# Layer norm, 32-head attention over one key/value head and an MLP on one core: one buffer for the transformed queries, a fifth set for VectorE's readings, the root by a power, and a new order

## The chip, the cores and the metric

One Trainium2 chip, one of its NeuronCores. The metric is the device time of one launch in microseconds (us), as the median of a few executions. The engines are TensorE (PE in the profile; PEld is its weight load), VectorE (DVE), ScalarE (ACT), GpSimd (POOL) and SyncE (SP, which issues most DMAs). TensorE writes to PSUM, which has eight banks of 512 float32 columns here.

## The reference

```python
def reference(A_x, A_wq, A_wk, A_wv, A_wo, B_x, B_w1, B_w2):
    x = A_x                                    # (1, 2048, 640), bfloat16
    xn = (x - mean(x)) / sqrt(var(x) + 1e-5)   # over the 640 columns
    q = (xn @ wq) as 32 heads of 20            # one key and one value head for all of them
    k, v = xn @ wk, xn @ wv                    # (2048, 20) each
    p = softmax(q k^T / sqrt(20)); o = p v
    return x + concat(o) @ wo + silu(xn @ w1) @ w2      # w1: 640x1728, w2: 1728x640
```

## The kernel before

The 2048 tokens are 16 tiles of 128 rows, and 4 query chunks of 512 columns. Everything is one static program: a list scheduler in the kernel file, run while the program is built, holds planned durations for every operation, plays the engines forward and writes out one list of instructions for each engine with semaphore waits between them. The tables of numbers at the top of the file (SEG, one row for each 32 blocks of work; PRO, the order of the opening jobs; ACT_STATS, NORM_ENG, DT, BATCHES) steer its choices. What stands on the chip is those lists, in their order.

**Opening.** The x tiles arrive by DMA (L1575). Mean and variance come from VectorE's bn_stats (L1685, L1687), or from two ScalarE passes with accumulators for the tiles in ACT_STATS (L1670, L1673, finished by two small VectorE steps, L1676 and L1680). A batch of tiles then gets 1/sqrt(var + eps) by two Newton steps on GpSimd: ten small instructions in a chain (L1734 to L1750), and two more where a GpSimd normalisation needs -mean/sqrt(...) (L1757, L1758). The batches are tiles 0-3, 4-9 and 10-15. The normalisation itself runs on VectorE (L1715) or GpSimd (L1711). Normalised tiles are transposed on TensorE (L1809, job tN) with a copy out by VectorE or ScalarE (L1820, L1817), or by a transposing DMA (L1775) for the tiles in DT. Then come key jobs k0 to k7 (L1828, evicted by L1836, with a second copy kT1 with an offset by GpSimd, L1838), value jobs v0 to v3 (L1851, L1860) and the first query jobs: p0 and p1 are the two halves of the first 128 query columns, q1 the next (all L872). While it waits, TensorE runs matmuls on zeros (L848, L839).

**Attention.** It is 2048 blocks of 128 keys by 512 queries (32 heads, 4 chunks, 16 key tiles). A visit to the scores, S (L1133), is three or four matmuls in 32-row tiles that run beside each other and fill three or four banks; what does not go together goes as one or two. For a block, either ScalarE takes the exponential (L1167, one instruction for one to three adjacent banks), or VectorE makes a 16-bit integer reading of it (L1182) that serves as the exponent bits of a bfloat16, and two shifted copies of this reading are made by integer additions, Y0 and Y1 (L1221 or L1227 on GpSimd, L1215 on VectorE). So a ScalarE block costs one matmul with v (PV, L973), and a VectorE block three. VectorE's readings lie in NZ = 4 sets of three blocks. PV matmuls run four beside each other in 32-column tiles: four matmuls are one slot. Before the wide integer addition is used, GpSimd loads another library (L1242).

**Other work.** Query, MLP and output jobs (L872) are cut into 32-column tiles too, four to a slot. A change of TensorE between row tiles, column tiles and whole-array matmuls is called a switch below. Transformed queries go through `qd` and DMAs (L1345) into qT, which has two buffers, one for even and one for odd chunks; both are first filled with offsets by one DMA each (L1787).

Of the kernel before, what the change touches and what calls it, by code (L numbers as in the profile page):

```python
# [16 lines left out]
P = 128  # L17
# [38 lines left out]
NZ = 4  # L56
# [5 lines left out]
H0_STEP = 10  # L62
# [25 lines left out]
FOUR_FROM = 35  # L88
# [7 lines left out]
PV_HOLD = 12  # L96
# [3 lines left out]
DT = (5, 6, 7, 8, 9, 10, 11, 12, 14, 15)  # L100
NORM_P = 0.9
# [14 lines left out]
K1_ENG = "pool"  # L116
PV_MIN = 3
PV_GO = 9
PRO = "t0 t2 t1 p0 t3 k0 k1 p1 q1 v0 t4 k2 v1 k3 k4 t13 v2 k5 k6 v3 k7 d0"
ACT_STATS = (1, 4, 6, 12, 14, 15)  # L120
NW_ENG = ("pool", "pool", "pool")
NORM_ENG = ("pool", "dve", "dve", "dve", "pool", "dve", "dve", "dve", "dve", "pool", "dve", "pool")
# [71 lines left out]
)  # L194
BATCHES = ((0, 4), (4, 10), (10, 16))
T_ACT = (0, 2, 6)


# [1742 lines left out]
```

## Time and profile before

| | us |
|---|---|
| median of 3 runs (lowest, highest) | 662.92 (662.53, 663.67) |
| the profiled execution, its own time | 662.48 |
| its span, first to last instruction | 660.7 |
| busy: TensorE, ScalarE, VectorE, GpSimd | 654.3, 645.8, 601.5, 420.3 |
| first scores matmul, from the span's start | 17.76 |

Times in the views are counted from the span's start. A busy share of TensorE counts overlapping matmuls once; the ends of matmuls are modelled, so the distance from start to start is the better measure of what one costs. Idle time is put down to the instruction whose end came last.

### The profile page before, as it was taken

To read this page: it belongs to the slowest core of one execution; us is meant where nothing else is said; L and a number is where in the kernel's file an instruction comes from. 1 tells how busy PE (TensorE), PEld (TensorE's weight loads), DVE (VectorE), ACT (ScalarE), POOL (GpSimd) and SP (SyncE) were. 2 spreads that over 40 slices of the span, in tenths; PEclk is the share of its full clock that TensorE was granted. 3 is DMA by queue.
4 is the path that set the end of the run, shared out by engine and by line. 5 is a ranking of instruction groups with operands and counts; after the bars stand their busy time and mean duration, and the time that the engine had idled before them with its cause. 6 is when DMAs were issued, how large, how long until landed. Compare 5 with 4: busy or idle time off the path is not lost.

```text
span 660.7 us, 22924 instructions
## 1 busy us (share of the span) xinstructions
PE 654.3 (99%) x9762; PEld 220.6 (33%) x9764; DVE 601.5 (91%) x1060; ACT 645.8 (98%) x735; POOL 420.3 (64%) x568
## 2 busy tenths in 40 slices
PE   8999999999999999999999999999999999999998
PEld 4432222323333333333333333333332333333334
DVE  7799999899999997999999979999999998999995
ACT  7899999999999999999999999999999999999995
POOL 6646667676776662676666744677666664766673
PEclk9999999999999999999999999999999999999999
DMA  7566300000004200001003210000000310011001
GB/s 212 97 237 195 88 18 11 10 13 13 14 20 72 73 10 10 10 10 18 18 11 57 63 39 10 18 10 8 12 19 10 77 55 25 10 18 34 11 10 42
DMA packets 52058, 27.89 MB, mean 42 GB/s; under 512 B 37910, under 2 KB 51318, under 8 KB 51958
## 3 DMA queue, kind: packets, MB, share of 16 engines
q1 hardware_dynamic: 50502, 26.22, 15.6%
q8 instruction: 78, 1.28, 0.8%
q10 hardware_dynamic: 1456, 0.22, 0.2%
q14 instruction: 22, 0.18, 0.1%
HBM read 11.44 MB, written 2.62 MB: 21 GB/s over the span
## 4 chain that ended last, share of the span: by engine, by line
PE 92%; ACT 3%; DVE 2%; DMA 2%; SPq 1%; issue 0%; DVEq 0%
PE psall L973 34%; PE psall L1133 29%; PE psall L872 27%; ACT sbt L1167 3%; DMA sbt<-sbt 1%; DVE sbt L1685 1%; DMA sbt<-in_A_x_dram 1%; SPq L1575 0%; DVE sbt L1715 0%; PE psall L1828 0%; PE psall L1369 0%; PE psall L1851 0%; ACT sbt L1379 0%; DVE sbt L1467 0%; DVE sbt L1820 0%
## 5 line engine op out<-in xcount | busy, mean ns | idle before, releaser
L1167 ACT ACTIVATE sbt<-psall 128x1024 bf16<-128x1024 f32 (+2 forms) x644 | 609.6, 1068 | 3.5 <-PE psall L1133 2.9
L1221 POOL INT64_ADD sbt<-sbt x491 | 394.1, 815 | 209.1 <-DVE sbt L1182 183.8
L1182 DVE TENSOR_SCALAR sbt<-psall 128x512 int16<-128x512 f32 x739 | 476.4, 684 | 37.1 <-PE psall L1133 27.6
L973 PE MATMUL psall<-sbt 128*32 128x512 bf16 x3526 | 266.7, 383 | 0.0
L1133 PE MATMUL psall<-sbt 32*128 32x512 bf16 x2048 | 243.6, 384 | 0.3 <-ACT sbt L1167 0.2
L872 PE MATMUL psall<-sbt 128*32 128x320 bf16 (+2 forms) x3939 | 218.3, 331 | 0.3 <-DVE sbt L1687 0.3
L1133 PEld LDWEIGHTS psall<-sbt 32*128 32x128 bf16 x2048 | 61.8, 91 | 235.2 <-issue 80.8
L872 PEld LDWEIGHTS psall<-sbt 128*32 128x32 bf16 x3939 | 85.6, 95 | 85.1 <-issue 50.2
L973 PEld LDWEIGHTS psall<-sbt 128*32 128x32 bf16 x3526 | 63.3, 95 | 99.5 <-issue 68.9
L1384 DVE SCALAR_TENSOR_TENSOR sbt<-sbt,psall 128x512 bf16<-128x512 bf16 x54 | 36.7, 682 | 6.5 <-ACT sbt L1379 6.0
L1379 ACT ACTIVATE sbt<-psall 128x512 bf16<-128x512 f32 x54 | 33.6, 629 | 0.4 <-PE psall L872 0.3
L1285 DVE CAST sbt<-psall 128x512 bf16<-128x512 f32 x32 | 21.9, 683 | 0.6 <-PE psall L973 0.4
L1275 DVE TENSOR_TENSOR sbt<-sbt 128x320 bf16<-128x320 bf16 x31 | 15.8, 510 | 0.0
L1448 DVE SCALAR_TENSOR_TENSOR sbt<-psall,sbt 128x320 bf16<-128x320 f32 x28 | 13.5, 484 | 1.6 <-PE psall L872 1.2
L848 PE MATMUL psall<-sbt 128*128 128x512 bf16 (+2 forms) x44 | 12.9, 447 | 1.4 <-DVE sbt L1624 1.2
L1467 DVE SCALAR_TENSOR_TENSOR sbt<-psall,sbt 128x320 bf16<-128x320 f32 x28 | 13.0, 482 | 1.2 <-PE psall L872 1.2
L1336 DVE TENSOR_SCALAR sbt<-psall 128x512 bf16<-128x512 f32 (+1 forms) x19 | 12.9, 678 | 0.1
L1685 DVE BATCH_NORM_STATS2 sbt<-sbt 128x6 f32<-128x320 bf16 x20 | 8.9, 471 | 3.4 <-DMA sbt<-in_A_x_dram 3.4
L1269 DVE RECIPROCAL sbt<-sbt 128x16 f32<-128x16 bf16 x31 | 7.6, 244 | 0.4 <-DMA sbt<-sbt 0.4
L848 PEld LDWEIGHTS psall<-sbt 128*128 128x128 bf16 x46 | 4.8, 112 | 7.5 <-issue 3.3
L1227 POOL TENSOR_TENSOR sbt<-sbt 128x768 int32<-128x768 int32 x4 | 5.9, 1465 | 0.5 <-DVE sbt L1182 0.5
L1464 ACT ACTIVATE sbt<-psall 128x320 bf16<-128x320 f32 x4 | 1.6, 437 | 4.4 <-PE psall L872 4.3
(72 smaller groups left out, 90.8 us busy)
## 6 DMA issues: line engine op xcount, KB each, us to landing
sbt<-in_A_x_dram SPq DMA_DIRECT2D x32, 160.0 KB, 3.7
out_dram<-sbt SPq DMA_DIRECT2D x15, 160.0 KB, 2.0
sbt<-in_B_w_dram SPq DMA_DIRECT2D x5, 432.0 KB, 5.3
sbt<-sbt SPq DMA_DIRECT2D x105, 20.0 KB
sbt<-in_B_w_dram SPq DMA_DIRECT2D x13, 160.0 KB, 3.0
sbt<-sbt SPq DMA_DIRECT2D x1, 1024.0 KB, 6.3
sbt<-sbt SPq DMA_TRANSPOSE x57, 2.5
sbt<-in_A_wo_dram SPq DMA_DIRECT2D x5, 160.0 KB, 3.0
```

What stands on the lines that cost most here:

```text
L848: return pe.matmul(self.bk(b, 0, n), self.zero[:, 0:P], self.zero[:, 0:n], start=True, stop=True)
L872: ins = pe.matmul(self.bk(b, 0, n, r, r + SLOT), w[:, r:r + SLOT], x, start=start, stop=stop, tile_position=(0, r), skip_group_check=True)
L973: ins = pe.matmul(self.bk(ub[k], 0, QW, r, r + SLOT), self.v[:, it.w, it.kt, :], it.x(), start=f, stop=False, tile_position=(0, r), skip_g ...
L1133: ins = pe.matmul(self.bk(bank[x]), self.kT[r:r + SLOT, kk, kt * P:(kt + 1) * P], self.qT[r:r + SLOT, g % 8, (g // 8) % 2, :], start=True, ...
L1167: return a.activation(self.E[:, b0 * QW:(b0 + na) * QW].rearrange("p (b n) -> p b n", n=QW), src, AF.Exp, scale=ACT_SCALE)
L1182: return v.tensor_scalar(self.Z[:, zs, zp * QW:(zp + 1) * QW], self.bk(bb), 0.0, ZMAX, ALU.max, ALU.min)
L1221: sc.new("pool", tp, lambda v, k=k, c=c: v.int64_add(self.Y[:, zs, k, 0:w].bitcast(I64), self.Z[:, zs, 0:w].bitcast(I64), c), zk + [("lib" ...
L1275: op = sc.new(eng, 0.067 + 16 * DH / 960.0, lambda v: v.tensor_tensor(dst, ut[:, :, :, 0:DH], rb, ALU.mult), [key, ("rL", up)], [("o", h0 ...
L1285: sc.new("dve", t_dve_ps(QW), lambda v: v.tensor_copy(self.U[:, up, :], self.bk(ub)), [("B", ub)], [("U", up)], prio=U_PRIO, name=f"Uev{g}")
L1379: sc.new("act", t_act(QW), lambda a: a.activation(t, src, AF.Tanh, scale=0.5), [("B", b)], [("tb", tp)], prio=TH_PRIO, name=f"th{c}_{fk}") ...
L1384: sc.new("dve", t_dve_ps(QW), lambda v: v.scalar_tensor_tensor(out=self.hT[0:rows, fk, :], in0=t, scalar=1.0, in1=src, op0=ALU.add, op1=AL ...
L1685: np_("dve", 0.41, lambda v, hf=hf: v.bn_stats(self.st6[:, n, hf, :], x[:, hf * 320:hf * 320 + 320]), self.xkeys(n), [("st6", n, hf)], pri ...
```

## The change

- qT has one buffer in place of two; the queries of the next chunk overwrite it head by head, and the second fill of 1024 KB (L1787) goes. A condition in the builder demands that every score that reads a head's old queries has been issued before the new ones are made.
- NZ is 5: VectorE's readings have a fifth set.
- 1/sqrt(var + eps) is an addition of eps and one power with exponent -0.5 on GpSimd (`root`), in place of ten Newton instructions. GpSimd's normalisation adds -mean and multiplies with the root, so that only a sign change of the mean (`nm`) is needed beside it. The batches become 0-1, 2-3, 4-7, 8, 9-10 and 11-15.
- kT1 is made by VectorE, GpSimd makes six normalisations instead of four, and GpSimd loads its library for the wide additions right after them (with K1_ENG = "dve", `go_wide` is called ahead of the jobs); the four narrow additions L1227 go.
- The two loads of wk and wv are issued by ScalarE after its table load, not before it. ACT_STATS has five tiles instead of six; tile 0, 1 and 3 now have theirs from VectorE.
- Seven tiles are transposed by TensorE and nine by DMA (before six and ten); all tables have new numbers, so the lists are in a new order.

```diff
-NZ = 4
+NZ = 5
-H0_STEP = 10
+H0_STEP = 15
-FOUR_FROM = 35
+FOUR_FROM = 25
-PV_HOLD = 12
+PV_HOLD = 16
-DT = (5, 6, 7, 8, 9, 10, 11, 12, 14, 15)
-NORM_P = 0.9
+DT = (4, 5, 7, 9, 10, 11, 12, 13, 15)
+NORM_P = 0.7
+POW_FIX = 0.45
+POW_COL = 0.145
+AG_NEXT = 3
-K1_ENG = "pool"
+K1_ENG = "dve"
-PRO = "t0 t2 t1 p0 t3 k0 k1 p1 q1 v0 t4 k2 v1 k3 k4 t13 v2 k5 k6 v3 k7 d0"
-ACT_STATS = (1, 4, 6, 12, 14, 15)
-NW_ENG = ("pool", "pool", "pool")
-NORM_ENG = ("pool", "dve", "dve", "dve", "pool", "dve", "dve", "dve", "dve", "pool", "dve", "pool")
+PRO = "t2 t0 t1 p0 t3 k0 k1 p1 q1 v0 k2 t6 k3 v1 t8 k5 k4 k6 t14 v2 k7 d0 v3"
+ACT_STATS = (2, 4, 6, 12, 15)
+NORM_ENG = ("pool", "pool", "dve", "dve", "pool", "dve", "dve", "dve", "pool", "dve", "pool", "pool")
-    (8.178, 1.808, 1.279, 0.2, 2, 4, 1, 2.527, 0.05, 0.93, 0.18, 32, 0.3, 0.573, 10, 6, 2, 54, 24, 30, 6, 0, 1, 0, 99, 0, 2, 0, -9),
+    (4.197, 1.591, 0.708, 0.165, 6, 5, 5, 0.922, 0.05, 0.3, 2.631, 29, 2.57, 0.576, 10, 21, 7, 54, 22, 33, 21, 0, 0, 0, 99, 0, 2, 0, 2.412),
...
-BATCHES = ((0, 4), (4, 10), (10, 16))
-T_ACT = (0, 2, 6)
+BATCHES = ((0, 2), (2, 4), (4, 8), (8, 9), (9, 11), (11, 16))
+T_ACT = (2, 4, 5, 6)
...
-        self.qT = sb([P, HT, 2, QW], BF16)
+        self.qT = sb([P, HT, QW], BF16)
...
+            assert c == 0 or self.bp >= GB * (8 * (c - 1) + (hi - 1) // DH // 4 + 1)
...
-                np_("pool", 0.85, lambda g: g.tensor_scalar(
-                    xa(n), self.xslot(n), self.rstd[:, n:n + 1], self.nb[:, n:n + 1], ALU.mult, ALU.add),
+                np_("pool", 0.87, lambda v: v.tensor_scalar(
+                    xa(n), self.xslot(n), self.nm[:, n:n + 1], self.rstd[:, n:n + 1], ALU.add, ALU.mult),
...
+        def root(a, b_, pr):
+            ve = self.tmp[:, 0, a:b_]
+            h = self.half[:, :]
+            hb = bass.AP(self.half, h.offset, [list(h.ap[0]), [0, b_ - a]])
+            add = np_("pool", 0.2, lambda g: g.tensor_scalar(ve, self.mv[:, a:b_, 1], EPS, None, ALU.add), mvk(a, b_),
+                      [("va", a)], prio=pr, name="eps")
+            add.then = np_("pool", POW_FIX + POW_COL * (b_ - a), lambda g: g.tensor_tensor(self.rstd[:, a:b_], ve, hb, ALU.pow),
+                           [("va", a), ("half",)], [("rs", a)], prio=pr, name="root")
+            add.lock = add.then.lock = True
+            if any(NORM_ENG[n - 4] == "pool" for n in range(max(a, 4), b_)):
+                np_("pool", 0.22, lambda g: g.tensor_scalar(self.nm[:, a:b_], self.mv[:, a:b_, 0], -1.0, None, ALU.mult),
+                    mvk(a, b_), [("nm", a)], prio=pr + 0.01, name="nm").lock = True
```

The lists at three places. TensorE from its first key job to the first scores, before (L1828 are keys, L848 matmuls on zeros, L872 with 256 columns is p1 and with 512 columns q1, L1133 scores):

```order
L1809 MATMUL psall<-sbt 128x128 x5
L1828 MATMUL psall<-sbt 128x256 x5
L848 MATMUL psall<-sbt 128x512
L1828 MATMUL psall<-sbt 128x256 x5
L872 MATMUL psall<-sbt 32x256 x20
L872 MATMUL psall<-sbt 32x512 x20
L1133 MATMUL psall<-sbt 128x512 x6
L1851 MATMUL psall<-sbt 128x20 x20
```

and the same stretch now (L1780, L1799, L851, L875 and L1136 are the lines that were L1809, L1828, L848, L872 and L1133; L1822 was L1851):

```order
L1780 MATMUL psall<-sbt 128x128 x5
L1799 MATMUL psall<-sbt 128x256 x5
L851 MATMUL psall<-sbt 128x512
L851 MATMUL psall<-sbt 128x448
L1799 MATMUL psall<-sbt 128x256 x5
L875 MATMUL psall<-sbt 32x256 x20
L851 MATMUL psall<-sbt 128x512
L851 MATMUL psall<-sbt 128x480
L875 MATMUL psall<-sbt 32x512 x4
L1136 MATMUL psall<-sbt 128x512 x5
L875 MATMUL psall<-sbt 32x512 x16
L1822 MATMUL psall<-sbt 128x20 x17
```

Two matmuls on zeros stand behind p1, and only the first of q1's five slots is ahead of the first scores; the other four stand behind them. Ahead of this stretch, tiles 2, 0 and 1 are transposed in one row of 15, where tile 0 came first and 2 and 1 followed after two matmuls on zeros.

GpSimd at the first root, before (L1780 makes the offsets that qT is filled with, L1734 to L1750 are the Newton chain):

```order
L1649 MEMSET sbt 128x16
L1780 TENSOR_SCALAR sbt<-sbt 128x512
L1734 TENSOR_SCALAR sbt<-sbt 128x4
L1735 TENSOR_SCALAR sbt<-sbt 128x4
L1741 TENSOR_TENSOR sbt<-sbt 128x4
L1748 TENSOR_TENSOR sbt<-sbt 128x4
L1749 TENSOR_SCALAR sbt<-sbt 128x4
L1750 TENSOR_TENSOR sbt<-sbt 128x4
```

and now (L1727 adds eps, L1729 is the power, L1653 and L1657 are small constants, L1754 is the line that was L1780):

```order
L1727 TENSOR_SCALAR sbt<-sbt 128x2
L1729 TENSOR_TENSOR sbt<-sbt 128x2
L1653 TENSOR_TENSOR sbt<-sbt 128x1
L1657 MEMSET sbt 128x16
L1754 TENSOR_SCALAR sbt<-sbt 128x512
L1727 TENSOR_SCALAR sbt<-sbt 128x2
L1729 TENSOR_TENSOR sbt<-sbt 128x2
```

The root of tiles 0 and 1 is ahead of the offsets, that of tiles 2 and 3 behind them; no library load (ISA in the list) stands ahead of a power.

TensorE some 100 blocks into the attention, before (L973 is PV):

```order
L1133 MATMUL psall<-sbt 128x512 x3
L973 MATMUL psall<-sbt 32x512 x8
L1133 MATMUL psall<-sbt 128x512 x3
L973 MATMUL psall<-sbt 32x512 x16
L1133 MATMUL psall<-sbt 128x512 x4
```

and now, at its first visit of four (L1136 scores, L976 PV):

```order
L1136 MATMUL psall<-sbt 128x512 x3
L976 MATMUL psall<-sbt 32x512 x8
L1136 MATMUL psall<-sbt 128x512 x4
L976 MATMUL psall<-sbt 32x512 x8
L1136 MATMUL psall<-sbt 128x512 x3
```

Visits of four blocks begin earlier, and there are more of them over the run.

More of the change, by code (lines that the diff above doesn't have):

```diff
@@ L549, in alloc @@
         self.eps = sb([P, 1], F32)
+        self.half = sb([P, 1], F32)
+        self.nm = sb([P, NT], F32)
         self.cy = sb([P, 2], I32)
@@ L697, in s_reads @@
             c, h = g // 8, 4 * (g % 8) + j
-            k += [("kT1" if x in dvs else "kT", kt // 2), ("kT", kt // 2), ("qb", c % 2, h)] + self.qkeys(c, h)
+            k += [("kT1" if x in dvs else "kT", kt // 2), ("kT", kt // 2), ("qb", 0, h)] + self.qkeys(c, h)
         return k
@@ L1351, in consume @@
                 op.inc_no = len(ops)
-        reads = [("xnT", 4 * c + i) for i in range(4)] + [("wqd", 0), ("wqd", 1), ("qz", c % 2)]
+        reads = [("xnT", 4 * c + i) for i in range(4)] + [("wqd", 0), ("wqd", 1), ("qz", 0)]
         if c >= 2:
@@ L1624, in prologue @@
         np_("dve", 0.3, lambda v: v.memset(self.zero[:, :], 0.0), [], [("zero",)], prio=-1.0, name="zero")
-        pool(0.1, lambda g: g.memset(self.eps[:, :], EPS), [], [("eps",)])
+        pool(0.1, lambda g: g.memset(self.half[:, :], -0.5), [], [("half",)])
         for k in range(2):
@@ L1684, in stats @@
             for hf in range(2):
-                np_("dve", 0.41, lambda v, hf=hf: v.bn_stats(self.st6[:, n, hf, :], x[:, hf * 320:hf * 320 + 320]),
-                    self.xkeys(n), [("st6", n, hf)], prio=prio, name=f"st{n}")
-            np_("dve", 0.10, lambda v: v.bn_aggr(self.mv[:, n, :], self.st6[:, n, :, :]),
-                [("st6", n, 0), ("st6", n, 1)], [("mv", n)], prio=prio - 0.001, name=f"ag{n}")
+                last = np_("dve", 0.41, lambda v, hf=hf: v.bn_stats(self.st6[:, n, hf, :], x[:, hf * 320:hf * 320 + 320]),
+                           self.xkeys(n), [("st6", n, hf)], prio=prio, name=f"st{n}")
+            op = np_("dve", 0.10, lambda v: v.bn_aggr(self.mv[:, n, :], self.st6[:, n, :, :]),
+                     [("st6", n, 0), ("st6", n, 1)], [("mv", n)], prio=prio - 0.001, name=f"ag{n}")
+            if n == AG_NEXT:
+                last.then = op
         def mvk(a, b_):
@@ L1766, in prologue @@
                 self.batch[n] = a
-            newton(a, b_, 0.001 * i if b_ <= 4 else 0.3, NW_ENG[i])
+            root(a, b_, 0.001 * i if b_ <= 4 else 0.3)
             if b_ <= 4:
@@ L1780, in prologue @@
         pool(0.95, lambda g: g.tensor_scalar(self.qo[:, :], self.zero[:, 0:QW], self.offq[:, :], 1.0, ALU.add, ALU.mult),
-             [("zero",), ("offq",)], [("qo",)])
+             [("zero",), ("offq",)], [("qo",)], 0.5)
         tb = self.qo[:, :]
-        def qz(par, extra=()):
-            h0 = 2 if par == 0 else 0
-            rep = bass.AP(self.qo, tb.offset, [list(tb.ap[0]), [0, HT - h0], list(tb.ap[1])])
-            op = sc.dma("sp", lambda q: q.dma_start(self.qT[:, h0:HT, par, :], rep), [("qo",)] + list(extra),
-                        [("qb", par, h) for h in range(4 * h0, H)], P * (HT - h0) * QW * 2, sem=sem(f"qz{par}"))
-            op.inc_no = 1
-            sc.note(op, (), [("qz", par)])
-        qz(0)
+        h0 = 2
+        rep = bass.AP(self.qo, tb.offset, [list(tb.ap[0]), [0, HT - h0], list(tb.ap[1])])
+        op = sc.dma("sp", lambda q: q.dma_start(self.qT[:, h0:HT, :], rep), [("qo",)],
+                    [("qb", 0, h) for h in range(4 * h0, H)], P * (HT - h0) * QW * 2, sem=sem("qz"))
+        op.inc_no = 1
+        sc.note(op, (), [("qz", 0)])
         if W1_LATE:
             load_w1()
-        pool(0.4, lambda g: g.memset(self.w2[:, FC, :], 0.0), [], [("w2z",)])
+        pool(0.4, lambda g: g.memset(self.w2[:, FC, :], 0.0), [], [("w2z",)], 0.5)
         def late_loads(key):
```

73 lines of the change are left out of this document (14 added, 59 removed), and 124 rows, old and new, of the table SEG.

## The prediction

> **What bounds the kernel now.** I read the busy shares first, then busy time by stretch, then single instructions in order of time. The page's first parts:
>
> ```profile
> span 660.7 us, 22924 instructions
> PE 654.3 (99%) x9762; PEld 220.6 (33%) x9764; DVE 601.5 (91%) x1060; ACT 645.8 (98%) x735; POOL 420.3 (64%) x568
> ```
>
> Two engines are nearly full. The stretches (TensorE, its weight load, VectorE, ScalarE, GpSimd, granted clock) tell when:
>
> ```profile
> 0.00:10.00 10.00, 8.83 (x29) 3.51 (x30) 5.69 (x20) 7.31 (x16) 7.39 (x33) 1.00 0.83 229
> 10.00:20.00 10.00, 9.30 (x133) 5.14 (x133) 10.00 (x39) 8.69 (x19) 4.63 (x18) 1.00 0.49 149
> 20.00:30.00 10.00, 9.11 (x101) 4.12 (x101) 7.55 (x20) 8.96 (x11) 6.87 (x20) 1.00 0.55 91
> 30.00:40.00 10.00, 9.70 (x131) 4.05 (x130) 8.79 (x21) 9.45 (x12) 6.95 (x7) 1.00 0.82 265
> 40.00:60.00 20.00, 20.00 (x274) 5.86 (x273) 19.30 (x34) 20.00 (x25) 9.47 (x13) 1.00 0.51 164
> ...
> 100.00:200.00 100.00, 99.90 (x1509) 32.03 (x1509) 94.19 (x159) 100.00 (x107) 71.33 (x88) 1.00 0.06 15
> ...
> 600.00:640.00 40.00, 40.00 (x636) 13.39 (x628) 37.48 (x65) 40.00 (x44) 28.74 (x36) 1.00 0.08 19
> ```
>
> From 40 us on both are at 99 to 100%; only the first 40 us leave TensorE idle, 1.9 us of it between 10 and 40. A busy TensorE may still hide waits inside its overlapping matmuls, so I look at starts, in the timeline of TensorE alone:
>
> ```profile
> 99.78 0.39 PE L973 MATMUL psall<-sbt 128*32 128x512 bf16 x4
> 100.10 0.39 PE L1133 MATMUL psall<-sbt 32*128 32x512 bf16 x3
> 100.42 0.62 PE L973 MATMUL psall<-sbt 128*32 128x512 bf16 x8
> 100.97 0.39 PE L1133 MATMUL psall<-sbt 32*128 32x512 bf16 x3
> ...
> 103.03 0.83 PE L973 MATMUL psall<-sbt 128*32 128x512 bf16 x12
> 103.80 0.40 PE L1133 MATMUL psall<-sbt 32*128 32x512 bf16 x4
> 104.12 0.61 PE L973 MATMUL psall<-sbt 128*32 128x512 bf16 x8
> ```
>
> A visit is followed by PV 0.32 us after its start, whether three scores were issued (100.10) or four (103.80). Rows of 4, 8 and 12 PV matmuls take 0.32, 0.55 and 0.77. So a slot of 512 columns costs 0.222, a visit 0.215, and each switch 0.105: 0.215 + 0.105 = 0.32; 2 x 0.222 + 0.105 = 0.55; 3 x 0.222 + 0.105 = 0.77. A slot of 320 columns follows from the last job:
>
> ```profile
> 654.96 2.63 PE L872 MATMUL psall<-sbt 128*32 128x320 bf16 x72
> ```
>
> Seventeen starts in 2.63 - 0.30 us (0.30 is one matmul's length, below) give 0.137.
>
> ```profile
> L872 PE MATMUL psall<-sbt 128*32 128x320 bf16 x2464 | 116.2, 302 | 0.0
> L1167 ACT ACTIVATE sbt<-psall 128x1024 bf16<-128x1024 f32 x577 | 544.5, 1054 | 2.9 <-PE psall L1133 2.5
> L1167 ACT ACTIVATE sbt<-psall 128x1536 bf16<-128x1536 f32 x44 | 65.1, 1484 | 0.5 <-PE psall L1133 0.4
> L1167 ACT ACTIVATE sbt<-psall 128x512 bf16<-128x512 f32 x23 | 14.2, 624 | 0.1
> L1182 DVE TENSOR_SCALAR sbt<-psall 128x512 int16<-128x512 f32 x739 | 476.4, 684 | 37.1 <-PE psall L1133 27.6 <-PE psall L973 0.5 <-POOL sbt L1221 0.3
> ```
>
> Counted over the order of before from its first scores on, TensorE has 621 visits, 1250 switches, 1251 slots of 512 columns, 616 of 320, and small whole-array work for some 8 us: 133.5 + 131.3 + 277.7 + 84.4 + 8 = 635. Measured from the first scores at 17.76 (below) to the last matmul's end at 657.59 it is 639.8. Rounding a price by 0.002 moves this by 2.5 us, and 1.9 are the early waits. So TensorE runs through its list almost without a stop: its list is the time. ScalarE is full beside it; were its work to grow, it would take over.
>
> **The change part by part: TensorE's list.** The new order has 613 visits (210 rows of four instead of 186), 1230 switches, 1259 slots of 512 columns and as many of 320. Of the eight slots more, three are PV: VectorE now reads 745 blocks instead of 739 (TENSOR_SCALAR instructions in its list), two more matmuls each. The other five are query work, four of them q1's, which stood ahead of the first scores. One tile more is transposed after them: five matmuls, 0.28 (ten took 0.73 from 12.17, five 0.45 from 11.45, below). Matmuls on zeros are about as many. In all -8 x 0.215 - 20 x 0.105 + 8 x 0.222 + 0.28 = -1.72 - 2.10 + 1.78 + 0.28 = -1.8 us.
>
> **The other engines' load.** ScalarE has 18 exponentials over two banks less, 11 over three more and 3 over one less. A two-bank one costs 544.5 / 577 = 0.944 us, a three-bank one 65.1 / 44 = 1.480, a one-bank one 14.2 / 23 = 0.617: -17.0 + 16.3 - 1.9 = -2.6 us, more than TensorE loses. VectorE gets six readings, 6 x 476.4 / 739 = 3.9 us, and eight copies kT1 that the trace shows on GpSimd only. Nearest on VectorE: a one-column step took 0.14 (L1680 at 12.91) and a normalisation of 640 columns 1.46 / 4 = 0.37, so 1.1 to 2.9 for eight, and I take 2. Against 601.5 busy of 660.7 that is under 1%; what hides it is VectorE's idle 59 us. GpSimd is 64% busy and loses work. Its library load now starts right after its normalisations and costs it one wait:
>
> ```profile
> POOL sbt L1242 <- issue: 8.5, 1, 8.5
> ```
>
> PV work of the first group covers it on both sides. One qT buffer adds no wait: a query job is made at the earliest Q_LEAD = 54 visits, 162 blocks, ahead of its use, so 512 - 162 = 350 blocks after the last score that reads the old queries, some 109 us at 639.8 us for 2048 blocks. The fifth set only loosens waits. Both at nothing; should a DMA be late, TensorE's list stops there, since it is in order, and every engine with it.
>
> **The opening.** Its steps before:
>
> ```profile
> 1.17 10.04 PE L848 MATMUL psall<-sbt 128*128 128x512 bf16 x34 [1.17 <-DVE sbt L1624]
> ...
> 4.05 0.72 ACT L1670 ACTIVATE sbt<-sbt 128x640 bf16<-128x640 bf16 x1
> ...
> 5.08 0.89 DVE L1685 BATCH_NORM_STATS2 sbt<-sbt 128x6 f32<-128x320 bf16 x2 [0.66 <-DMA sbt<-in_A_x_dram]
> ...
> 5.54 0.19 ACT L1673 ACTIVATION_READ_ACCUMULATOR sbt<-sbt 128x1 f32 x1
> ...
> 6.36 0.69 POOL L1780 TENSOR_SCALAR sbt<-sbt 128x512 bf16<-128x512 bf16 x1
> ...
> 7.97 0.26 POOL L1734 TENSOR_SCALAR sbt<-sbt 128x4 f32<-128x4 f32 x1 [0.93 <-DVE sbt L1687]
> ...
> 8.56 0.49 DVE L1685 BATCH_NORM_STATS2 sbt<-sbt 128x6 f32<-128x320 bf16 x1 [0.32 <-DMA sbt<-in_A_x_dram]
> ...
> 10.55 0.20 POOL L1750 TENSOR_TENSOR sbt<-sbt 128x4 f32<-128x4 f32 x1
> ...
> 11.00 1.46 DVE L1715 TENSOR_SCALAR sbt<-sbt 128x640 bf16<-128x640 bf16 x4
> ...
> 11.45 0.45 PE L1809 MATMUL psall<-sbt 128*128 128x128 bf16 x5 [0.23 <-DVE sbt L1715]
> ...
> 12.17 0.73 PE L1809 MATMUL psall<-sbt 128*128 128x128 bf16 x10
> ...
> 12.91 0.13 DVE L1680 TENSOR_SCALAR sbt<-sbt 128x1 f32<-128x1 f32 x1
> ...
> 16.02 1.81 PE L872 MATMUL psall<-sbt 128*32 128x256 bf16 x40
> ...
> 16.80 0.47 ACT L1313 ACTIVATE sbt<-psall,sbt 128x256 bf16<-128x256 f32 x1
> ...
> 17.76 0.60 PE L1133 MATMUL psall<-sbt 32*128 32x512 bf16 x6
> ```
>
> Ten Newton steps run from 7.97 to 10.75, then four normalisations, the transposes from 11.45, p1 and q1 from 16.02, ScalarE's eviction of p1 at 16.80, and scores at 17.76, behind q1. Now I follow the new lists with these durations. ScalarE reads tile 2, which lands at 5.08 (VectorE waited for it), in 1.7 us (two passes and two read-outs took from 4.05 to 5.73), so VectorE has its variance at 7.3. GpSimd does the first root at about 6.2, then the offsets (0.69), and starts the second root at 8.1. The power is in no row. Below it can't be under a small GpSimd addition, 0.20 (10.55); above, I let it cost the whole chain, 2.78. I take 0.7, nearer to the small instruction, since it is one of them with more arithmetic. Then the second root ends at 9.1. VectorE normalises tiles 0 and 1 from 7.4, has five readings of tiles 5 and 7 to do (tile 7 lands at 8.56), and normalises 2 and 3 from 9.95. The transposes start at 10.45 instead of 11.45. The matmuls on zeros that stand ahead of them are six fewer, 1.3 us, and cover this to 0.5 us.
>
> From there VectorE copies tiles 0 and 1 out between readings, p0 starts at 12.5, k1 after VectorE's copy of tile 3 at 14.65, p1 at 15.3 (16.02 before), its eviction ends at 16.5, and the first scores start at 16.75: **-1.0 us**. With a power of 0.2 they start no earlier, for VectorE's readings hold tile 2; if all other waits shrink too, -2.0. With 2.78, two of them in a row and the offsets between, tile 2 is normalised at 13.5 and the first scores come at 20.3: +2.5. The early waits of 1.9 us stay, between 0.9 (the transposing DMAs are one fewer and start earlier) and 2.9.
>
> **The sum.** 660.7 - 1.8 - 1.0 = 657.9 of span; the profiled execution took 662.48, so 1.8 more, 659.7. The median is 0.4 above that execution: **660.1 us**, I say 660.0.
>
> **The rivals.**
> - *The opening gains nothing.* The later x tiles set it: tile 7 lands at 8.56 and TensorE waits for transposing DMAs after the first scores. For it: VectorE is 100% busy from 10 to 20 us, and the new lists give it more readings there. Then -1.8 alone or, with one more us of early waits, -0.8: 661 to 662.3, between faster and no change.
> - *Slower: the fourth bank.* Twenty-four more visits hold four banks at once, and TensorE, in order, waits until the engines have emptied them. Weight loads for scores wait on VectorE and ScalarE already, up to 0.5 us at a time, but under running matmuls:
>
> ```profile
> PEld psall L1133 <- DVE sbt L1182: 69.7, 175, 0.4
> PEld psall L1133 <- ACT sbt L1167: 42.5, 106, 0.5
> ```
>
>   If each of the 24 stood still for 0.4 us (69.7 / 175), that is 9.6: 669.6. It counts as slower from 4.2 / 24 = 0.18 each. Against it: 186 visits of four leave TensorE at 100% now, and ScalarE's load falls.
> - *Slower: the power needs code of its own.* The row of L1242 shows 8.5 us for a library. Were a load hidden in the first power, the second root would end near 15.7, the first scores come 4.9 later than before and the sum be 662.9 - 1.8 + 4.9 = 666.0; it decides from about 4 us on. Against it: the lists have an instruction of their own ahead of each library load, and none ahead of a power; the first addition and the last product of the Newton chain took 0.26 and 0.20 (7.97, 10.55), no sign of a load. [...]
>
> **How the numbers follow.** A measurement of this kernel tells about 0.2% from no change, 1.3 us: faster is under 661.6, slower over 664.2. The forecast case has 0.74 and lies at 657.5 to 661.5 (first scores -2.0 to 0, early waits 0.9 to 1.9, switch price 0.1). The first rival has 0.14, half faster and half the same; the fourth bank 0.08; the code load 0.04. So faster 0.74 + 0.07 = 0.81, same 0.07, slower 0.12. The range, 657.5 to 664.0, holds the first two cases and the dear power without code load, and leaves out the slower ones.
>
> **What would show it.** Right: first scores near 16.75, transposes near 10.45, a power under 1 us, TensorE at 100% from 40 us on, and 641 us from the first scores to the end (642.9 before). Wrong: TensorE under 99% in a stretch after 40 us, with score weight loads that wait longer than 0.5 us; or a power of over 2.8 us.

## The result: 2.5 us faster, and the profile after

The changed kernel takes 660.41 us in the median of 20 executions (658.93 to 662.90), the kernel before 662.93 in as many (661.70 to 664.80): a ratio of 0.9963, 95% interval 0.9954 to 0.9973. The forecast was 660.0 in a range from 657.5 to 664.0. The profiled execution of the changed kernel took 659.94 (before 662.48), its span 658.1 (660.7). Two parts of its page, busy time and the costliest groups:

```profile
span 658.1 us, 22878 instructions
PE 649.4 (99%) x9776; PEld 221.9 (34%) x9778; DVE 604.4 (92%) x1075; ACT 642.1 (98%) x721; POOL 417.9 (63%) x543
...
L1170 ACT ACTIVATE sbt<-psall 128x1024 bf16<-128x1024 f32 (+1 forms) x634 | 608.7, 1077 | 4.3 <-PE psall L1136 3.5
```

TensorE lost 4.9 us of busy time and ScalarE 3.7, VectorE gained 2.9. The timeline of the opening, all engines, with the rows that answer to those of before (L1727 adds eps, L1729 is the power, L1719 normalises on VectorE, L1780 transposes, L875 with 256 columns is p0 and p1, L1136 are scores):

```profile
6.08 0.26 POOL L1727 TENSOR_SCALAR sbt<-sbt 128x2 f32<-128x2 f32 x1
6.42 0.74 POOL L1729 TENSOR_TENSOR sbt<-sbt 128x2 f32<-128x2 f32 x1
7.20 1.21 DVE L1719 TENSOR_SCALAR sbt<-sbt 128x640 bf16<-128x640 bf16 x2 [0.24 <-POOL sbt L1729]
...
8.79 0.71 POOL L1729 TENSOR_TENSOR sbt<-sbt 128x2 f32<-128x2 f32 x1
...
10.46 1.01 PE L1780 MATMUL psall<-sbt 128*128 128x128 bf16 x15 [1.57 <-DVE sbt L1719]
...
12.26 0.73 PE L875 MATMUL psall<-sbt 128*32 128x256 bf16 x20
...
14.83 0.73 PE L875 MATMUL psall<-sbt 128*32 128x256 bf16 x20
...
15.61 0.47 ACT L1316 ACTIVATE sbt<-psall,sbt 128x256 bf16<-128x256 f32 x1
...
16.35 0.60 PE L1136 MATMUL psall<-sbt 32*128 32x512 bf16 x5
```

The transposes begin at 10.46 and the first scores at 16.35, 1.41 us earlier than before. TensorE's own timeline shows its two main stops afterwards, early at k6 (L1799) and once near the end:

```profile
29.52 0.39 PE L1136 MATMUL psall<-sbt 32*128 32x512 bf16 x3
31.17 0.71 PE L1799 MATMUL psall<-sbt 128*128 128x256 bf16 x5 [1.26 <-DMA sbt<-sbt]
31.81 0.39 PE L1136 MATMUL psall<-sbt 32*128 32x512 bf16 x3
...
637.88 0.83 PE L976 MATMUL psall<-sbt 128*32 128x512 bf16 x12
639.18 0.40 PE L1136 MATMUL psall<-sbt 32*128 32x512 bf16 x4 [0.47 <-ACT sbt L1170]
```

The same in its stretches (TensorE, weight load, VectorE, ScalarE, GpSimd, granted clock):

```profile
30.00:40.00 10.00, 8.76 (x112) 3.55 (x113) 8.74 (x21) 8.54 (x10) 2.20 (x4) 1.00 0.86 317
40.00:60.00 20.00, 19.96 (x285) 6.49 (x286) 18.95 (x35) 19.85 (x25) 13.22 (x17) 1.00 0.44 127
...
600.00:640.00 40.00, 39.51 (x605) 13.03 (x601) 37.34 (x65) 39.30 (x42) 28.39 (x37) 1.00 0.08 19
```

Where the 2.6 us of span come from is read best from the starts of single scores matmuls in the two traces (L1133 before, L1136 after; the last row but one is the last matmul of all):

```
start of                 before    after   difference
first scores              17.76    16.35      -1.41
129th scores matmul       62.07    61.69      -0.38
1921st scores matmul     613.07   609.70      -3.37
last matmul              657.29   654.75      -2.54
end of the span          660.7    658.1       -2.6
```

Beside it stands the list alone, each instruction at the prediction's prices in the order of the lists: 638.1 us before, 636.1 after, so -2.0 (the prediction's count by groups gave 635 before; rounding moves both sums alike). Of that, +0.4 lies ahead of the 129th scores matmul (42.6 and 43.0) and -2.4 behind it. So up to there -1.41 + 0.4 + 0.63 more of waits = -0.38; from there on -2.4 of list and 0.2 more of waits. Most of what the opening won was spent again by 62 us. Part of the 1.41 was never a gain: four slots of q1, 4 x 0.222 = 0.9 us, moved from ahead of the first scores to behind them. From the first scores to the last matmul the time fell by 1.1 us (639.5 to 638.4): -2.0 of list, +0.8 of waits, the rest rounding.

### The profile page after: what moved, and what is told of

Its sections match the earlier page's. It is cut to its first block, busy times and chain, and to the rows that moved or that the text cites. A ratio compares the mean times of both kernels' runs of the same rounds, so it can differ in the third digit from the quotient of the medians.

```text
span 658.1 us, 22878 instructions
## 1 busy us (share of the span) xinstructions
PE 649.4 (99%) x9776; PEld 221.9 (34%) x9778; DVE 604.4 (92%) x1075; ACT 642.1 (98%) x721; POOL 417.9 (63%) x543
## 3 DMA queue, kind: packets, MB, share of 16 engines
HBM read 11.44 MB, written 2.62 MB: 21 GB/s over the span
## 4 chain that ended last, share of the span: by engine, by line
PE 95%; DVE 1%; POOL 1%; ACT 1%; DMA 1%; issue 0%; DVEq 0%; SPq 0%; POOLq 0%
PE psall L976 35%; PE psall L1136 30%; PE psall L875 28%; ACT sbt L1170 1%; DMA sbt<-sbt 1%; PE psall L851 1%; DVE sbt L1185 0%; PE psall L1799 0%; PE psall L1373 0%; DVE sbt L1719 0%; POOL sbt L1715 0%; DVE sbt L1693 0%; PE psall L1780 0%; PE psall L1822 0%; POOL sbt L1655 0%
## 5 line engine op out<-in xcount | busy, mean ns | idle before, releaser
L1170 ACT ACTIVATE sbt<-psall 128x1024 bf16<-128x1024 f32 (+1 forms) x634 | 608.7, 1077 | 4.3 <-PE psall L1136 3.5
L1224 POOL INT64_ADD sbt<-sbt x494 | 399.1, 820 | 215.3 <-DVE sbt L1185 185.9
L976 PE MATMUL psall<-sbt 128*32 128x512 bf16 x3538 | 267.7, 383 | 0.0
L1136 PE MATMUL psall<-sbt 32*128 32x512 bf16 x2048 | 240.3, 384 | 1.4 <-ACT sbt L1170 0.5
L875 PE MATMUL psall<-sbt 128*32 128x320 bf16 (+2 forms) x3939 | 213.4, 330 | 0.1
L1136 PEld LDWEIGHTS psall<-sbt 32*128 32x128 bf16 x2048 | 61.2, 91 | 234.2 <-issue 97.1
L875 PEld LDWEIGHTS psall<-sbt 128*32 128x32 bf16 x3939 | 86.3, 96 | 82.4 <-issue 45.6
L976 PEld LDWEIGHTS psall<-sbt 128*32 128x32 bf16 x3538 | 63.2, 95 | 100.9 <-issue 70.2
L851 PE MATMUL psall<-sbt 128*128 128x512 bf16 (+3 forms) x41 | 11.4, 422 | 1.3 <-DVE sbt L1632 1.2
L1799 PE MATMUL psall<-sbt 128*128 128x256 bf16 x40 | 5.7, 272 | 1.3 <-DMA sbt<-sbt 1.3
L851 PEld LDWEIGHTS psall<-sbt 128*128 128x128 bf16 x43 | 4.2, 107 | 6.5 <-issue 2.6
L1678 ACT ACTIVATE sbt<-sbt 128x640 bf16<-128x640 bf16 x5 | 3.7, 732 | 2.8 <-DMA sbt<-in_A_x_dram 2.6
```

What stands on the lines that cost most here:

```text
L851: return pe.matmul(self.bk(b, 0, n), self.zero[:, 0:P], self.zero[:, 0:n], start=True, stop=True)
L875: ins = pe.matmul(self.bk(b, 0, n, r, r + SLOT), w[:, r:r + SLOT], x, start=start, stop=stop, tile_position=(0, r), skip_group_check=True)
L976: ins = pe.matmul(self.bk(ub[k], 0, QW, r, r + SLOT), self.v[:, it.w, it.kt, :], it.x(), start=f, stop=False, tile_position=(0, r), skip_g ...
L1136: ins = pe.matmul(self.bk(bank[x]), self.kT[r:r + SLOT, kk, kt * P:(kt + 1) * P], self.qT[r:r + SLOT, g % 8, :], start=True, stop=True, ti ...
L1170: return a.activation(self.E[:, b0 * QW:(b0 + na) * QW].rearrange("p (b n) -> p b n", n=QW), src, AF.Exp, scale=ACT_SCALE)
L1224: sc.new("pool", tp, lambda v, k=k, c=c: v.int64_add(self.Y[:, zs, k, 0:w].bitcast(I64), self.Z[:, zs, 0:w].bitcast(I64), c), zk + [("lib" ...
```

## The experiments

All comparisons are with the changed kernel (660.41; 660.42 in a second series) unless said otherwise; ratios are to the kernel before on the same chip. The planner's order was held fixed in all but the last two.

**The power alone, taken out and put in.** In the changed kernel the power was replaced by the nine small instructions of the Newton chain (the edit, shortened):

```diff
-            add.then = np_("pool", ..., lambda g: g.tensor_tensor(self.rstd[:, a:b_], ve, hb, ALU.pow),
+            add.then = np_("pool", ..., newt,        # bit trick, then twice: y*y, *v, *-0.5+1.5, *y
```

> The changed kernel with its order of instructions held fixed on every engine, and only the power taken back: each of the six roots is an addition and nine dependent small GpSimd instructions (the Newton chain, about 2.8 us) instead of an addition and one power (0.74 us for two columns). Theory (the power moves the opening, TensorE's list carries the rest unchanged): the root of tiles 0 and 1 ends near 8.8 instead of 7.2, the offsets (0.69) come behind it, the root of tiles 2 and 3 ends near 12.3 instead of 9.5, the first transposes start near 12.8 instead of 10.46, and the first scores come near 18.7 instead of 16.35. The end comes later by those 2.3 us, or by up to 2 more where the later roots delay the transposing transfers that k6 waits for: 662.7 to 664.7 us against 660.4. Rival (the opening gains nothing, since the early waits give back what the first scores gain): within 0.7 us of 660.4, with the first scores late and the waits between 17 and 36 us smaller by as much.

669.84 us (668.34 to 671.96; ratio 1.0090, 1.0069 to 1.0111): 9.4 more, outside both theories. TensorE's timeline (L1794 are transposes, L1813 keys; the row at 29.79 is k2):

```profile
13.41 1.78 PE L1794 MATMUL psall<-sbt 128*128 128x128 bf16 x15 [4.62 <-DVE sbt L1719]
...
21.30 0.60 PE L1136 MATMUL psall<-sbt 32*128 32x512 bf16 x5
...
29.79 1.22 PE L1813 MATMUL psall<-sbt 128*128 128x256 bf16 x5 [3.53 <-DMA sbt<-sbt]
...
33.14 0.61 PE L1136 MATMUL psall<-sbt 32*128 32x512 bf16 x3
```

and its stretches, where the granted clock is the column behind GpSimd's:

```profile
12.00:14.00 2.00, 0.59 (x6) 0.59 (x7) 1.09 (x5) 0.00 (x0) 0.63 (x4) 0.50 0.72 246
14.00:16.00 2.00, 2.00 (x15) 1.44 (x13) 1.58 (x6) 1.42 (x3) 0.00 (x0) 0.50 0.00 0
...
38.00:40.00 2.00, 2.00 (x15) 1.07 (x12) 1.75 (x4) 1.02 (x1) 0.00 (x0) 0.50 0.45 99
```

The roots delay the transposes by 2.95 us, near the 2.3 expected. Two things come on top. The later roots are late too, for which the expectation allowed up to 2 us: the first transposing DMA is issued 6.79 us later (SyncE's timeline, the changed kernel and, below, this one):

```profile
16.50 13.86 SPq L1749 DMA_TRANSPOSE sbt<-sbt  x9
```

```profile
23.29 9.16 SPq L1763 DMA_TRANSPOSE sbt<-sbt  x5
```

k2, which doesn't wait in the changed kernel, waits 3.53 us for a transposing DMA. The other I had not in mind: with the waits the clock goes. TensorE runs at half its clock from 10.9 to 17.7 (a visit of three takes 0.61, not 0.39), and again from 28.0 to 41.6. The first scores come 4.95 late, the 41st scores matmul 11.6 in this execution (the slowest of the six, 671.96), and the distance stays 11.6 until the late waits. Of the 11.6, the transposes are 2.95, the clock up to the first scores 2.0, and k2's wait in place of the changed kernel's at k6 2.2 (3.53 - 1.35, its second profile below). The 4.5 that are left I put down to the clock behind k2, by subtraction; so somewhat more than half is the clock.

The reverse, the kernel before with the power in its first root only (the edit in words):

```diff
-  ten GpSimd instructions for the root of tiles 0 to 3
+  eps added, then one power of four columns
```

> The kernel before with its order of instructions held fixed, and only the first root (tiles 0 to 3) made by a power: an addition and one power of four columns (about 1.03 us by the changed kernel's rows) in place of ten small instructions that ran from 7.97 to 10.75. Theory (the power alone gains next to nothing, the new order is needed to use it): the root is done near 9.3, but VectorE's readings of other tiles stand ahead of the four normalisations in its list until 10.97, so these start at 11.00 as before; first scores at 17.5 to 17.8, time within 0.4 us of 662.9. Rival (the chain of small instructions was the bound of the opening): normalisations from 9.6, first scores 1.4 us earlier, 661.5 us.

662.85 (ratio 0.9994, 0.9979 to 1.0008): no gain. VectorE's timeline has the four normalisations (L1732) right behind the reading of another tile, 1.2 us after the power had ended (GpSimd: start 8.59, 1.06 long):

```profile
9.98 0.83 DVE L1702 BATCH_NORM_STATS2 sbt<-sbt 128x6 f32<-128x320 bf16 x2
10.73 0.19 DVE L1704 BATCH_NORM_AGGREGATE sbt<-sbt 128x2 f32<-128x12 f32 x1
10.84 1.46 DVE L1732 TENSOR_SCALAR sbt<-sbt 128x640 bf16<-128x640 bf16 x4
```

So the power is worth nothing in the old order and 9.4 us in the new one: the new order puts two roots and GpSimd's offsets in a row and needs short roots. What an order that was planned for Newton chains from the start would lose was not tried.

**Does TensorE's list hold the time, and alone?** First, less work for ScalarE:

```diff
+                cut = QW if v < 120 else 448      # exponentials on 448 of 512 columns
```

> The changed kernel, its order fixed, with the exponentials of all but the first 120 visits made on 448 of each block's 512 columns (an eighth of the exponentials is left out); TensorE does all that it did. ScalarE's two-block exponential should fall from 1.08 us by about 0.11, some 45 to 50 us over the run. Theory (TensorE's list is the time): 659.4 to 660.4, TensorE still at 99 to 100%, the idle time of ScalarE larger by as much as its work shrinks; only the late waits of about 1 us can go. Rival (ScalarE, busy 98%, is the bound or nearly so): 640 or less.

660.56 (ratio 0.9957, 0.9941 to 0.9973): no gain, as the list theory says. An exponential over two banks takes 0.92 us instead of 1.05, but ScalarE's busy time falls only by 23.8 (642.1 to 618.3), about half of what was expected. Then less for TensorE:

```diff
+                cut = QW if f else 448            # PV matmuls on 448 of 512 columns
```

> The changed kernel, its order fixed, with all PV matmuls but each group's first row made on 448 of 512 columns (an eighth of the weighted sum of values is left out). By the price of a slot (0.222 us for 512 columns, that is 64 columns = 0.027) some 858 slots get shorter, 22.9 us in all. Theory (TensorE's list is the time, and a slot costs what its columns cost): 18 to 23 us less, 637.5 to 642.5, less the full 22.9 where ScalarE, whose exponentials start to start add up to some 613 us, becomes the next bound. Rival (a slot's price is not its columns, or another engine is the bound): 660.

657.39 (ratio 0.9921, 0.9906 to 0.9937): 3.0 less, not 18 to 23. The theory that TensorE's list is the time *alone* falls. The slots did get shorter as expected: two of them and a switch take 0.495 us from start to start in the median, where the changed kernel has 0.548,

```profile
104.24 0.56 PE L977 MATMUL psall<-sbt 128*32 128x448 bf16 x8
104.74 0.39 PE L1137 MATMUL psall<-sbt 32*128 32x512 bf16 x3
```

so a slot is 0.027 shorter, some 23 us over the run, and the list is about 613 us. But from the first scores to the last matmul 634.3 went by, so some 21 us of waits came in where the changed kernel has 2.3. One stretch of each shows it, the changed kernel and, below, this one:

```profile
100.00:200.00 100.00, 99.90 (x1528) 32.23 (x1529) 94.71 (x160) 100.00 (x107) 69.64 (x87) 1.00 0.08 17
```

```profile
100.00:200.00 100.00, 99.08 (x1548) 33.97 (x1540) 95.09 (x161) 100.00 (x108) 69.97 (x87) 1.00 0.10 18
```

ScalarE was at 100% and stays there. Its busy share counts overlapping instructions once, so I look at starts here too: an exponential over one, two or three banks takes 0.477, 0.904 or 1.330 us from start to start in both traces, and with such prices ScalarE's work between 100 and 600 us fills 487 of 500 us in the changed kernel and 489 here. It has little room to follow a faster TensorE. Both cuts at once:

> The changed kernel, its order fixed, with both cuts of the two experiments before at once: exponentials on 448 of 512 columns after the first 120 visits, and PV matmuls on 448 columns (an eighth of exponentials and of the weighted sum is left out). The exponentials alone gained nothing (660.6), the matmuls alone 3 us (657.4), though TensorE's slots had become 27 us shorter by their prices. Theory of two tied engines (TensorE's list is the time and ScalarE stands right behind it, each hides a gain of the other): together they give most of the 27, 633 to 645 us. Rival (a third limit, VectorE's readings or the banks' round trips, holds the time): 652 to 657, as with the matmuls alone.

648.84 (ratio 0.9780, 0.9766 to 0.9795): 11.6 less, between the two forecasts. Of the 27 us in the expectation, starts show 23: the 27 goes by a price for 448 columns that the trace doesn't bear out. Its executions had a mean clock of 0.994 to 0.995 (1.000 is the full clock), and the profile shows half the clock from 31.7 to 38.6 us behind a wait of 1.60 at k6, 3.6 us of delay at the 129th scores matmul against the cut of PV alone. In the same stretch as above:

```profile
100.00:200.00 100.00, 99.37 (x1548) 33.29 (x1540) 96.07 (x163) 97.56 (x109) 70.86 (x88) 1.00 0.07 17
```

So TensorE and ScalarE are tied, and each alone hides a cut of the other. What keeps the last 8 to 11 us of the cut is open: no engine is at 100% here (TensorE 99.37, ScalarE 97.56, VectorE 96.07), and VectorE's readings were not cut.

**The waits.** Two places of TensorE's list were altered, k6 behind the next visit and tile 14's transposes, and one PV row ahead of the visit that waits at 639.18 (the orders, in words):

```diff
-  PV x4, scores x3, k6 x5, scores x3, t14 x5, v2 x20        -  PV x12, scores x4, PV x8
+  PV x4, scores x3, scores x3, t14 x5, k6 x5, v2 x20        +  PV x16, scores x4, PV x4
```

> The changed kernel with two places of TensorE's list altered and nothing else. First, the five matmuls of k6, which waited 1.26 us at 31.17 for their transposing transfer, go behind the next visit of scores and the transposes of tile 14: some 0.65 us of work then stands in the wait, and two switches of 0.105 go. Second, one row of the PV matmuls behind the visit of four at 639.18, which waited 0.47 us for an exponential, goes ahead of it (0.22). Theory (TensorE's list with its few waits is the whole time): 0.6 to 1.1 us less than the changed kernel, 659.3 to 659.8, with the waits at these places smaller by as much. Rival (the waits belong to banks and exponentials, and reappear at the next visit): no change, 660.4, with the same sum of waits at other rows.

660.31 (ratio 0.9957, 0.9942 to 0.9972): no change that can be measured. The rival was right for k6; in TensorE's timeline its wait of 1.26 turned into two (L1163 are scores, L1807 transposes, L1826 k6, L1849 v2):

```profile
30.49 0.40 PE L1163 MATMUL psall<-sbt 32*128 32x512 bf16 x3 [0.56 <-ACT sbt L1197]
30.82 0.45 PE L1807 MATMUL psall<-sbt 128*128 128x128 bf16 x5
31.11 0.71 PE L1826 MATMUL psall<-sbt 128*128 128x256 bf16 x5
32.34 0.66 PE L1849 MATMUL psall<-sbt 128*128 128x20 bf16 x20 [0.52 <-DVE sbt L1834]
```

The earlier visit waits for its banks, and v2 for k6's eviction (L1834). The visit after that starts at 33.02 instead of 33.08. The second place gained a little: the last matmul starts at 654.45 instead of 654.75.

**The clock and the matmuls on zeros.** Ten more of them, in the two longest waits (the edit in words):

```diff
+        extra = {first transposes: 6 matmuls on zeros, k6: 4 matmuls on zeros}
```

> The changed kernel, its order fixed, with ten more matmuls on zeros on TensorE and nothing else: six ahead of the first transposes (TensorE stood idle there from 8.89 to 10.46) and four ahead of k6 (idle from 29.9 to 31.17). They lie in waits, so the order theory expects the same time in an execution at full clock, 659.0 to 660.5. Clock theory, from the two experiments before (idle stretches of 3.5 to 4.6 us, and one of 1.39, were followed by 2.6 to 13 us at half the clock; the changed kernel's executions with a mean clock of 0.995 took 662.6 to 662.9, those at 1.000 took 658.9 to 660.5): with the waits filled, the executions below 0.999 go, the median is 659.7 to 660.2 and the highest under 661.5. Rival (the clock falls for reasons outside these two waits): 3 or 4 executions in 10 stay at 661.3 to 662.9.

> The changed kernel once more, on the same chip as the kernel with the added matmuls on zeros, for the spread of its executions: 660.4 in the median, some 4 in 10 with a mean clock under 0.999 and at 661.3 to 662.9. If the profiled execution is one of those, it shows at which wait the clock falls: by the clock theory right behind the wait at 9 to 10.5 or that at 30 to 31.2.

660.26 (659.51 to 660.51) and, for the changed kernel beside it, 660.42 (659.83 to 662.85, one of seven at a clock of 0.995). The profiled execution of the latter was at full clock; its idle stretch ahead of the transposes was 0.55, not 1.57, though the transposes began at 10.46 again, so the matmuls on zeros take another time from one execution to the next. They start 0.43 us apart until the clock first rises and 0.22 apart afterwards, and it rises at 4.26 in the one profile and at 6.32 in the other. The six added ones overran the wait: transposes at 11.37, first scores at 17.22, 0.88 later than in that second profile; at the last matmul 0.28 of it is left. Once more, and the opposite, six matmuls on zeros fewer:

> The kernel with ten more matmuls on zeros once more, for the spread: the first five executions were all at a mean clock of 0.999 or 1.000 (659.5 to 660.5), while 9 of the changed kernel's 27 were under 0.998. Clock theory: again all at or over 0.999, none above 661. Rival (chance): some 3 in 10 at 661.3 to 662.9.

> The changed kernel, its order fixed, with six fewer matmuls on zeros ahead of the first transposes, so that TensorE stands idle from about 7.5 to 10.46 instead of from 8.89. Clock theory: an idle stretch near 3 us is followed by half the clock for some us, as 4.6 us were; the opening to the first scores and what follows takes 2 to 5 us longer, 662.5 to 665, with a granted clock near 0.5 in the stretch after 10 us in the profile. Rival (the matmuls on zeros only fill time): 660.4, clock 1.00.

With ten more: 660.71 (659.74 to 660.93), again none below 0.999; of the changed kernel's 27 executions 9 were below 0.998. With six fewer: 662.80 (660.79 to 664.28; ratio 0.9984, 0.9972 to 0.9997, where the kernel with ten more had 0.9951, 0.9939 to 0.9964, beside the same runs of before), and all ten executions at 0.994 to 0.997. TensorE's timeline and three stretches of this kernel:

```profile
1.18 6.66 PE L859 MATMUL psall<-sbt 128*128 128x512 bf16 x22 [1.18 <-DVE sbt L1640]
10.46 1.01 PE L1788 MATMUL psall<-sbt 128*128 128x128 bf16 x15 [2.62 <-DVE sbt L1727]
...
17.89 0.60 PE L1144 MATMUL psall<-sbt 32*128 32x512 bf16 x5
...
31.39 0.72 PE L1807 MATMUL psall<-sbt 128*128 128x256 bf16 x5
```

```profile
10.40:11.60 1.20, 1.14 (x17) 1.03 (x18) 1.20 (x5) 1.07 (x4) 0.00 (x0) 0.99 1.06 367
11.60:13.00 1.40, 1.40 (x8) 0.31 (x10) 1.40 (x7) 0.77 (x3) 0.12 (x1) 0.50 0.99 316
13.00:15.00 2.00, 2.00 (x28) 1.30 (x23) 0.85 (x4) 0.82 (x2) 1.83 (x4) 0.50 0.29 104
```

The transposes start on time, but half the clock from 11.6 to 15 makes the first scores 1.54 late. This execution, the fastest of the ten, lost little by it: k6 (L1807 here) starts at 31.39, 0.12 behind the changed kernel's second profile, its wait gone. The six matmuls on zeros are thus worth some 2 us of the median (2.4 against the changed kernel, 2.1 against the kernel with ten more on the same chip), by the clock that they keep up: at a mean clock of 0.995 this kernel and the changed one both take 662.9 in the median. The ten more make the time steadier, not lower. If the rate of 9 in 27 held, none in ten would come by chance about once in 60 times, an estimate; on the one chip that ran both kernels the changed one had only one in seven. No kernel here that does the whole work is measurably faster than the changed one.

**The fifth set and the visits of four, undone one at a time.** Here the planner writes a new order.

```diff
-NZ = 5
+NZ = 4
```

> The changed kernel with four sets for VectorE's readings instead of five, everything else as changed. The planner then writes another order: 627 visits of scores instead of 613, 1262 switches instead of 1230, 1299 slots of 512 columns instead of 1259, by the prices of the prediction a list of 654.3 us against 636.1. Theory (the list is the time): 18.2 us more than the changed kernel, 677 to 680 us. Rival (the fifth set matters by the waits that it takes away, and the counts do not add up to the time): within 5 us of 660, or far above 680 with TensorE waiting.

690.03 (ratio 1.0413, 1.0398 to 1.0428): 29.6 more, of which the list explains 18.2. From the first scores to the last matmul 667.9 us pass for a list of 654.3, so waits are 13.6 instead of 2.3, and they grow with the length of the run (5.5 at the middle of the scores). One stretch:

```profile
200.00:300.00 100.00, 99.12 (x1563) 35.53 (x1564) 89.14 (x151) 93.53 (x105) 58.91 (x74) 1.00 0.11 28
```

ScalarE and VectorE have room there, against 100 and 95 in the changed kernel's stretch above. And part of the list is itself waiting. L842 are matmuls on zeros, which the planner puts where it expects TensorE to wait (the changed kernel and, below, this one):

```profile
L842 PE MATMUL psall<-sbt 128*32 128x512 bf16 x1 | 0.4, 379 | 0.0
```

```profile
L842 PE MATMUL psall<-sbt 128*32 128x512 bf16 (+7 forms) x40 | 11.9, 339 | 0.0
```

At a slot's price the 39 more are 8.7 of the 18.2 us. With the 11.3 of other waits (13.6 - 2.3), about 20 of the 29.6 us are waits, planned for or not; the 14 visits and 32 switches more are 6.4 by price. So the rival was right in large part: the fifth set matters by the waits that it takes away. And the limit for visits of four:

```diff
-FOUR_FROM = 25
+FOUR_FROM = 35
```

> The changed kernel with visits of four scores allowed from the 35th on as before, instead of the 25th; the planner writes another order, with 629 visits instead of 613 and 1265 switches instead of 1230: by the prices a list of 644.7 us against 636.1. Theory (the list plus waits like the changed kernel's): 669 us; with waits that grow as with four sets (the list 18 us longer, the time 30), up to 676. Rival (a visit of four costs more than a visit of three, so fewer of them are no loss): 660 or less.

675.79 (ratio 1.0192, 1.0169 to 1.0215): 15.4 more, 8.6 of list and 6 to 8 of waits. Both say that a table made for one setting loses under another, by more than its visits and switches. They don't say what the setting is worth to a planner tuned for it. Two qT buffers together with five sets were not tried, so what the one buffer is worth by itself is not shown.

## Why the prediction was right, step by step

- **The list, -1.8.** By the same prices over the full lists it is -2.0, and starts and prices part by only 1.5 us before and 2.3 after. But the 0.8 more of waits count: from the first scores to the last matmul the trace has -1.1. And "its list is the time" was too much: some 23 us off the PV slots gained 3.0. That the term came out here I put down to ScalarE's work falling as well: the prediction had -2.6, by starts it is -3.1 (18 x 0.904 and 3 x 0.477 less, 11 x 1.330 more), and busy time fell from 645.8 to 642.1. No run has the shorter list without ScalarE's relief, so this is argued, not shown. The reading "ScalarE is full beside it" stood in the prediction; that it would hold back a shorter list did not.
- **VectorE's copies kT1 at 2.** The eight take 2.1 together. (The one-column step that the prediction took as 0.14 is 0.13 in its row, which changes nothing.)
- **The power at 0.7.** 0.74, 0.71 and 0.73 for two columns, 0.58, 1.03 and 1.19 for one, four and five. The first, at 6.42, costs 0.74, what the later ones do, so there is no load of code in it, and that rival falls. The upper bound, the dear power of 2.78, was mis-sized: the prediction put the first scores at 20.3 by it, 3.5 behind its forecast, and counted that case inside the range. The Newton chain in its place put them at 21.30 and cost 9.4, a time of 669.84, since neither the later transposing DMAs nor the clock were in the term.
- **The opening, -1.0.** Normalisation of tiles 2 and 3 from 9.97 (forecast 9.95), transposes 10.46 (10.45), p0 12.26 (12.5), p1 14.83 (15.3), first scores 16.35 (16.75): -1.41. The early waits didn't stay at 1.9: 0.63 more by the 129th scores matmul, above all at k6, so -0.8. The mechanism of the first rival was at work, TensorE waits for transposing DMAs: the kernel with fewer matmuls on zeros has first scores 1.54 later and k6 0.12 later. Its time, 661 or more, wasn't reached, since 0.8 of the opening's gain was left and the list gave its -2.0.
- **"Cover this to 0.5 us".** True of one profile (0.55), not of the other (1.57); which of the two it is goes with the moment at which the clock first rises (6.32 and 4.26), so that part was luck. It was taken to cost nothing, and mostly did; a third of the executions had less than full clock (9 of 27 were below 0.998), and the kernel with ten more had none in ten.
- **The fourth bank.** It shows at one visit of four, 0.47 at 639.18 (0.32 in the second profile), where the stretch falls under the 99% named as a sign of being wrong (39.51 of 40) and a score weight load waited 0.9 us, the longest in its row:

```profile
PEld psall L1136 <- DVE sbt L1185: 71.1, 176, 0.4
PEld psall L1136 <- ACT sbt L1170: 39.0, 95, 0.9
```

  Before, those rows had 69.7 and 42.5. Not 24 stops of 0.4, but some half a microsecond. Undoing the earlier start of visits of four made the kernel slower.
- **Fifth set and one buffer at nothing.** The waits listed for the changed kernel name neither. But the set isn't free to take away: in this order's tables it is worth 29.6 us, some 20 of them waits. What it gives is the order that the planner can write, which was in the count of the list.
- **From the first scores to the end, 641.** 658.1 - 16.35 = 641.75. The sum: -2.0 - 0.8 + 0.2 = -2.6 against -2.8. That it is so close owes something to luck: the first scores come 0.4 earlier than forecast, and the stretch behind them is shorter by 1.1, not 1.8.

## What to carry to other kernels

Count an in-order engine's list with prices read from starts, and the difference of two lists was good to about a microsecond here (-2.0 by the list, -1.1 by the trace, new waits between); but what such an engine would gain by itself can be capped by the next engine (here 3.0 of some 23 us off the PV slots, with ScalarE at 100% from 100 to 200 us), and a cut of its work says by how much. When an opening gets faster, look for the wait that ends last behind it (here the transposing DMA ahead of k6), not for the first step that moves. And price a delay of a few microseconds on TensorE with the clock that it loses, not only with its own length: here transposes that came 2.95 us later put the 41st scores matmul 11.6 late, and somewhat more than half of that is the clock.

## What the hardware showed that I had not expected

- Half the granted clock came in or behind waits of 4.62 and 3.53 us, but also of 2.62, 1.60 and 1.39 (the last in the kernel before with the power, at 30.95). Waits of 1.57, 1.35 and 1.26 in the changed kernel's two profiles left it at 1.00, so the length of a wait alone doesn't decide. Half the clock then lasted 3.41 us (with 1.39 and 2.62), 6.83 (with 1.60 and 4.62) or 13.65 (with 3.53), that is one, two and four times 3.41. With Newton chains the full clock between the two halved stretches, from 17.72 to 27.96, is three times 3.41, and in the clock records of before and after it lasts 655.36 us, 192 times 3.413, from a first rise that comes at 6.38 us after the span's start in the one and at 4.26 in the other. One or two times 3.41 us at half the clock make a mean clock of 0.997 or 0.995 over 660 us, an estimate; the changed kernel's executions at these two took 661.1 to 661.7 and 662.6 to 662.9, those at 0.999 and over 658.9 to 661.0. The stretches of the kernel before with the power:

```profile
30.00:31.00 1.00, 0.04 (x2) 0.08 (x3) 0.00 (x0) 1.00 (x3) 1.00 (x1) 1.00 0.31 60
31.00:32.00 1.00, 1.00 (x23) 0.87 (x24) 0.31 (x2) 0.51 (x2) 0.28 (x1) 0.71 0.60 137
32.00:33.00 1.00, 1.00 (x5) 0.28 (x3) 0.44 (x2) 0.00 (x0) 0.00 (x0) 0.50 0.73 164
```

- A power on GpSimd costs about 0.43 us and 0.15 for each column of 128 rows in the changed kernel: 0.58 for one, 1.19 for five.
- Behind the 41st scores matmul the kernels with the same list keep their distance from the changed kernel's second profile to a few hundredths of a microsecond up to the late waits: with Newton chains 11.62 at the 41st and 11.60 at the 1981st, with ten more matmuls on zeros 0.68 and 0.67.
